# Four products by zero columns in each second block of an attention backward loop

## The chip, the cores and the metric

The kernel runs on one core of one Trainium2 chip. The metric is the device time of one execution, in microseconds. Before the change it is 2607.16 us, the median of 7 runs (2601.39 to 2613.71).

## The reference

The kernel computes a transformer block with adaptive layer norm and all its gradients: attention with 32 heads of 16 over 2048 tokens of width 512, a dense part with a squared ReLU (width 1792), in bfloat16. What matters here is the attention and its gradient:

```
scores = jnp.einsum('bhqd,bhkd->bhqk', q, k) * Dh ** (-0.5)
p = _softmax(scores, axis=-1)
o = jnp.einsum('bhqk,bhkd->bhqd', p, v)
...
_out, _vjp = jax.vjp(_f, A_x, A_wqkv, A_wo, B_w1, B_b1, B_w2, B_b2, c, w_mod)
_grads = _vjp(grad_out)
```

The gradient needs, for each head, dV (the transposed probabilities by dO), dS (the probabilities times dO by V transposed, less a row sum), dK (dS transposed by Q) and dQ (dS by K).

## The kernel before

The program runs three stages: forward (to about 1060 us of the profile), the gradient of the last dense chunk (to about 1180), and from there the backward loop of the attention, to about 2475. A short last stage makes the gradients of the input and of the qkv weights.

The backward loop works in units. A unit is one group of four heads, one stretch of 512 keys and one tile of 128 queries: 8 x 4 x 16 = 512 units. Four units that share their keys and lie in the same stretch of 512 queries are a block; there are 128. In each unit:

- `score` (L1546): for each of four heads a product of 32 rows (a head's 16 values and the row that carries the softmax's correction, padded) by 512 keys, into one of three PSUM banks, A, B or C. Bank C is the tag `px`, which is shared with others.
- `expo` (L1552): ScalarE exponentiates a bank of scores into `E_u`.
- `dp_pair` (L1564, L1566): for two heads TensorE makes dO by V transposed into `psD_u`, and VectorE multiplies that by `E_u` into `dS_u`. There are two such pairs in a unit, so 1024 in the loop.
- `transpose_unit` (L1579): a DMA turns `dS_u` into the tile `dsT`, which dQ needs.
- `k_quad` (L1597) and `v_quad` (L1606): four products each, one for each head, on four column tiles beside each other. They add to dK and dV, which stand in one PSUM bank, `accVK`, in rows 32 x head and on. A bank is summed over the 16 units of a stretch of keys, and then copied out by ScalarE (L1609).
- `dq_quad` (L1624) and `dq_out` (L1637): once for each block, two blocks later, the products for dQ into a bank that again has the tag `px`.

In every second block (`on_pe`) the last unit's `dS_u` is turned by TensorE instead of the DMA: `pe_turn` (L1587) makes eight turns of 128 x 128 into `ptT`, once for each half of the unit. Its bank has the tag `px` too, with one buffer. ScalarE then copies the bank into `dsT` (L1695). The second turn can so begin only when the copy of the first is done, and the next score in bank C only when the copy of the second is done.

The order of the work on TensorE, ScalarE and VectorE in a block is written out by hand as a string of tokens (`order_t` for a block with turns in it, `order_n` for one without): s is a score, e an exponential, D a `dp_pair`, q a `k_quad` or `v_quad` in turn, t a turn, T its copy, d two `dq_quad`, Q a `dq_out`. The loop at L1667 reads the tokens and issues in their order; each engine then works its own queue in order and waits on semaphores. The two strings take turns, so the pattern repeats after two blocks: a pair of blocks, of which there are 64.

The tile `KS_tok` (K by token) is 528 wide; its columns 512 to 527 are set to zero ahead of the loop (L1314), so that the last head's 32-column slice is whole. `dOs_tok` is dO by token.

Of the kernel before, what the change touches and what calls it, by code (L numbers as in the profile page):

```python
# [21 lines left out]
D = 512  # L22
DC = 4
H = 32
DH = 16
# [5 lines left out]
QPAD = 528  # L31
# [3 lines left out]
def kernel(  # L35
# [17 lines left out]
    PE = nc.tensor  # L53
# [91 lines left out]
    with ExitStack() as ph:  # L145
# [1006 lines left out]
        def head_fill(i):  # L1152
            for key in ("k", "v", "q", "do"):
                POOL.memset(hsets[i][key][:], 1.0 if key in ("k", "v") else 0.0)
# [333 lines left out]
    KS_tok, dOs_tok = keep["KS"], keep["dOs"]  # L1488
# [11 lines left out]
    with ExitStack() as ph:  # L1500
# [6 lines left out]
        NU = len(units)  # L1507
        hst, bst, sst, dqt, cur = {}, {}, {}, {}, {}

        def load_head(hg):  # L1510
            st = dict(hsets[hg % 2])
            st["qz"] = qz[hg % 2]
            st["acc"] = stg.tile([P, n], F32, name="dQacc", tag="dQacc", bufs=1)
            st["dq"] = stg.tile([P, n], BF, name="dQst", tag="dQst", bufs=1)
            st["vk"] = stg.tile([P, n], BF, name="vkb", tag="vkb")
            hst[hg] = st
# [22 lines left out]
        def score(u, hq, bank):  # L1539
            hg, kc, qc, qi = units[u]  # L1540
            st = hst[hg]
            qt = qc * 4 + qi
            r = 32 * hq
            psS = psx.tile([P, 512], F32, name=f"psS_{bank}", tag=banks[bank])
            sst[u, hq] = psS
            PE.matmul(psS[:], st["q"][r:r + 32, qt * P:(qt + 1) * P], st["k"][r:r + 32, kc * 512:kc * 512 + 512],  # L1546
                      start=True, stop=True, tile_position=(r, 0))

        def expo(u, hq):
            if hq == 0:  # L1550
                bst[u] = [ework.tile([P, 4, 512], BF, name="E_u", tag="E_u"), None]
            ACT.activation(bst[u][0][:, hq, :], sst.pop((u, hq))[:], AF.Exp, scale=SCALE)  # L1552

        def dp_pair(u, pair):
            hg, kc, qc, qi = units[u]
            st = hst[hg]
            qt = qc * 4 + qi
            if pair == 0:
                bst[u][1] = ework.tile([P, 4, 512], BF, name="dS_u", tag="dS_u", bufs=6)
            E_u, dS_u = bst[u]  # L1560
            psD = psd.tile([P, 2, 512], F32, name="psD_u", tag="pd")
            for hi in range(2):
                r = 32 * (2 * pair + hi)
                PE.matmul(psD[:, hi, :], st["do"][r:r + 32, qt * P:(qt + 1) * P], st["v"][r:r + 32, kc * 512:kc * 512 + 512],  # L1564
                          start=True, stop=True, tile_position=(r, 0))
            DVE.tensor_tensor(dS_u[:, 2 * pair:2 * pair + 2, :], psD[:], E_u[:, 2 * pair:2 * pair + 2, :], ALU.mult)  # L1566
            if qi == 3 and on_pe(u // 4):
                held["dS"] = dS_u

        def on_pe(b):  # L1570
            return b % 2 == 1

        def transpose_unit(u):
            hg, kc, qc, qi = units[u]
            if qi == 0:
                dqt[u // 4] = tpool.tile([P, 4, 16, P], BF, name="dsT", tag="dsT")
            if qi == 3 and on_pe(u // 4):
                return
            SP.dma_start(out=dqt[u // 4][:, qi], in_=bst[u][1].rearrange("p h k -> p (h k)"), transpose=True)  # L1579

        held = {}

        def pe_turn(b, half):
            pt = psx.tile([P, 8, P], BF, name="ptT", tag="px")
            for i in range(8):
                kt = i % 4
                PE.transpose(pt[:, i, :], held["dS"][:, 2 * half + i // 4, kt * P:(kt + 1) * P], identb[:])  # L1587
            dst = dqt[b][:, 3, 8 * half:8 * half + 8, :]
            held[half] = (dst, pt)
# [26 lines left out]
        def dq_quad(b, kt):  # L1616
            hg, kc, qc, _ = units[4 * b]
            if kt == 0:
                cur["dq"] = psx.tile([P, 512], F32, name="dqacc", tag="px")
            acc = cur["dq"]  # L1620
            tT = dqt[b]
            for hq in range(4):
                h = hg * 4 + hq
                PE.matmul(acc[32 * hq:32 * hq + 32, :], KS_tok[:, kc * 4 + kt, h * DH:h * DH + 32], tT[:, :, hq * 4 + kt, :],  # L1624
                          start=(kt == 0), stop=(kt == 3), tile_position=(0, 32 * hq), skip_group_check=True)

        def dq_out(b):
            hg, kc, qc, _ = units[4 * b]
            acc = cur["dq"]
            del dqt[b]  # L1630
            st = hst[hg]
            dst = st["acc"][:, qc * 512:(qc + 1) * 512]
            if kc == 0:
                ACT.activation(dst, acc[:], AF.Identity, scale=SCALE)
            else:
                tmp = wk.tile([P, 512], F32, name="dqtmp", tag="dqtmp")
                ACT.activation(tmp[:], acc[:], AF.Identity, scale=SCALE)  # L1637
                if kc == QC - 1:
                    dst2 = st["dq"][:, qc * 512:(qc + 1) * 512]
                else:  # L1640
                    dst2 = dst
                POOL.tensor_tensor(dst2, dst, tmp[:], ALU.add)  # L1642
            if kc == QC - 1 and qc == QC - 1 and hg < HG - 1:
                for hq in range(4):
                    r = hg % 2 * 64 + hq * DH
                    at(cur["j"] + 6 + hq, load, dQc[hg // 2, r:r + DH, :], st["dq"][32 * hq:32 * hq + DH, :])

        order_t = (
            "s0 s1 q s2 e0 e1 D s3 D e2 s4 e3 t1 e4 q T1 D "
            "s5 s6 e5 t2 e6 s7 T2 e7 D s8 e8 D s9 e9 q q s10 "  # L1650
            "s11 e10 D d1 d2 e11 Q q s12 D e12 s13 e13 q s14 D e14 "
            "s15 q q e15 ").split(), "ABCABBABACABABCA"
        order_n = (
# [9 lines left out]
        with tc.manual_schedule(engines={PE.engine, ACT.engine, DVE.engine, SP.engine, POOL.engine}):  # L1663
            head_fill(1)
            POOL.memset(qz[1][:], 0.0)
            nD, nq = -1, -4
            for b in range(NU // 4 + 3):  # L1667
                toks, bank = order_t if on_pe(b - 1) else order_n
                for tok in toks:
                    c, i = tok[0], int(tok[1:] or 0)  # L1670
                    if c == "s" and b < NU // 4:
                        if i == 0 and units[4 * b][1:] == (0, 2, 0) and units[4 * b][0] + 1 < HG:
                            load_head(units[4 * b][0] + 1)
                        score(4 * b + i // 4, i % 4, bank[i])
                    elif c == "e" and b < NU // 4:
                        expo(4 * b + i // 4, i % 4)
                    elif c == "D":
                        if 0 <= nD < 2 * NU:
                            dp_pair(nD // 2, nD % 2)
                            if nD % 2 == 1:  # L1680
                                transpose_unit(nD // 2)
                        nD += 1
                        cur["j"] = nD
                        for j in sorted(j for j in todo if j <= nD):
                            for f, args in todo.pop(j):
                                f(*args)
                    elif c == "q":
                        if 0 <= nq < 2 * NU:
                            (v_quad if nq % 2 else k_quad)(nq // 2)
                        nq += 1  # L1690
                    elif c == "t" and 0 <= b - 1 < NU // 4:
                        pe_turn(b - 1, i - 1)
                    elif c == "T" and 0 <= b - 1 < NU // 4:
                        dst, pt = held.pop(i - 1)
                        ACT.activation(dst, pt[:], AF.Identity)  # L1695
                    elif c == "d" and 0 <= b - 2 < NU // 4:
                        for kt in (2 * i - 2, 2 * i - 1):
                            dq_quad(b - 2, kt)
                    elif c == "Q" and 0 <= b - 2 < NU // 4:
                        dq_out(b - 2)  # L1700
            assert not todo
# [284 lines left out]
```

## Time and profile before

| what | value |
|---|---|
| median of 7 runs | 2607.16 us |
| the profiled execution | 2607.46 us, of which the profile's span is 2605.7 us |
| TensorE (PE) busy | 2352.8 us, 90% of the span |
| ScalarE (ACT) busy | 2304.6 us, 88% |
| VectorE (DVE) busy | 1809.8 us, 69% |
| the backward loop, first turn's copy to last pair's | 1202.2 to 2473.6 us |
| busy in that stretch of 1271.4 us | PE 1178.1, ACT 1211.5, DVE 1168.3 us |
| TensorE's granted clock in that stretch, mean | 0.93 of full speed |
| the copies of the turns, L1695 | 128 of 1.15 us |
| the turns, L1587 | 1024 products of 128 columns |

A share over the whole span says little here, since the stages have different limits: ahead of the loop VectorE is half idle, and in the loop three engines are each busy for nine tenths or more. In such a loop the order in which they wait for one another sets the time. The profile writes a group of instructions as its line, engine and operation, then output<-inputs; a matmul's form is written rows*columns of the part of the array that it uses, then the moving operand. Durations of matmuls overlap one another: how fast they follow is read from their starts. The clock of TensorE is given as a share of full speed.

### The profile page before, as it was taken

To read this page: it belongs to the slowest core of one execution; us is meant where nothing else is said; L and a number is where in the kernel's file an instruction comes from. 1 tells how busy PE (TensorE), PEld (TensorE's weight loads), DVE (VectorE), ACT (ScalarE), POOL (GpSimd) and SP (SyncE) were. 2 spreads that over 40 slices of the span, in tenths; PEclk is the share of its full clock that TensorE was granted. 3 is DMA by queue.
4 is the path that set the end of the run, shared out by engine and by line. 5 is a ranking of instruction groups with operands and counts; after the bars stand their busy time and mean duration, and the time that the engine had idled before them with its cause. 6 is when DMAs were issued, how large, how long until landed. Compare 5 with 4: busy or idle time off the path is not lost.

```text
span 2605.7 us, 49454 instructions
## 1 busy us (share of the span) xinstructions
PE 2352.8 (90%) x18444; PEld 758.6 (29%) x18444; DVE 1809.8 (69%) x2301; ACT 2304.6 (88%) x3565; POOL 363.6 (14%) x371
## 2 busy tenths in 40 slices
PE   7995989888989889898999999999999999999999
PEld 2231123222322222442222222222222222222243
DVE  5551354445344535579998999899999999999862
ACT  5996999999999999738999999999999999999952
POOL 4000010210242123201111101111011110100100
PEclk8885569997998899999999999899999999999999
DMA  3566565346847674989999999999999999999972
GB/s 130 153 160 172 160 146 134 107 119 130 139 85 150 138 123 93 240 237 198 196 193 193 197 201 200 189 201 195 200 197 197 199 194 197 194 192 209 189 249 73
DMA packets 1227775, 447.49 MB, mean 172 GB/s; under 512 B 1103419, under 2 KB 1198399, under 8 KB 1227278
## 3 DMA queue, kind: packets, MB, share of 16 engines
q1 hardware_dynamic: 1199614, 409.47, 80.1%
q0 software_dynamic: 10944, 16.78, 4.5%
q10 hardware_dynamic: 16976, 18.07, 2.5%
q8 instruction: 145, 2.38, 0.4%
q14 instruction: 96, 0.79, 0.1%
HBM read 96.75 MB, written 73.95 MB: 66 GB/s over the span
## 4 chain that ended last, share of the span: by engine, by line
PE 45%; ACT 36%; issue 6%; DVE 6%; DMA 2%; SPq 2%; POOL 1%; ACTq 0%; DVEq 0%; POOLq 0%
ACT E_u L1552 20%; ACT ET L555 11%; PE dqacc L1624 6%; PE psST L553 4%; PE psS_A L1546 4%; ACT dsT L1695 3%; PE accVK L1597 3%; PE psS_C L1546 3%; PE oacc L569 2%; PE psS_B L1546 2%; PE pm L228 2%; PE accVK L1606 2%; PE pm L393 2%; SPq L173 2%; PE pdh L1810 2%
## 5 line engine op out<-in xcount | busy, mean ns | idle before, releaser
L1566 DVE TENSOR_TENSOR dS_u<-psD_u,E_u 128x1024 bf16<-128x1024 f32 x1024 | 1187.3, 1218 | 105.9 <-PE psS_B L1546 50.7
L555 ACT ACTIVATE ET<-psST 128x1024 bf16<-128x1024 f32 x1024 | 946.4, 1171 | 69.8 <-PE psST L553 69.1
L1552 ACT ACTIVATE E_u<-psS_A 128x512 bf16<-128x512 f32 x768 | 504.4, 657 | 22.2 <-PE psD_u L1564 10.3
L1552 ACT ACTIVATE E_u<-psS_B 128x512 bf16<-128x512 f32 x768 | 500.0, 651 | 6.6 <-PE psS_A L1546 1.7
L1564 PE MATMUL psD_u<-iv,ido 32*128 32x512 bf16 x2048 | 424.1, 399 | 1.7 <-DVE dS_u L1566 1.5
L553 PE MATMUL psST<-qt_sb,kt_sb 32*128 32x512 bf16 x2048 | 353.5, 434 | 70.2 <-ACT ET L555 40.5
L1552 ACT ACTIVATE E_u<-psS_C 128x512 bf16<-128x512 f32 x512 | 333.1, 651 | 0.7 <-PE psS_B L1546 0.5
L1546 PE MATMUL psS_B<-ik,iq 32*128 32x512 bf16 x768 | 306.5, 399 | 10.8 <-ACT E_u L1552 3.4
L1546 PE MATMUL psS_A<-ik,iq 32*128 32x512 bf16 x768 | 304.5, 397 | 11.6 <-ACT E_u L1552 1.3
L569 PE MATMUL oacc<-ET,vaug 128*32 128x512 bf16 x2048 | 232.7, 444 | 5.2 <-DVE ostage L573 5.1
L1597 PE MATMUL accVK<-dS_u,qz 128*32 128x512 bf16 x2048 | 227.8, 414 | 0.3 <-DVE dS_u L1566 0.2
L1546 PE MATMUL psS_C<-ik,iq 32*128 32x512 bf16 x512 | 194.7, 380 | 33.0 <-ACT dsT L1695 29.0
L1546 PEld LDWEIGHTS <-iq 32*128 32x128 bf16 x2048 | 127.5, 92 | 312.1 <-issue 297.6
L1606 PE MATMUL accVK<-E_u,dOs_tok 128*16 128x512 bf16 x2048 | 211.5, 403 | 0.0
L1642 POOL TENSOR_TENSOR dQacc<-dQacc,dqtmp 128x512 f32<-128x512 f32 x64 | 81.2, 1269 | 879.5 <-ACT dqtmp L1637 879.5
L1624 PE MATMUL dqacc<-dsT,KS_tok 128*32 128x512 bf16 x2048 | 183.2, 467 | 12.2 <-DMA dsT<-dS_u 3.0
L553 PEld LDWEIGHTS <-kt_sb 32*128 32x128 bf16 x2048 | 86.7, 93 | 361.1 <-issue 327.2
L246 DVE COPY part<-pm 128x512 f32<-128x512 f32 (+2 forms) x103 | 63.5, 616 | 134.9 <-PE pm L228 131.0
L1695 ACT ACTIVATE dsT<-ptT 128x1024 bf16<-128x1024 bf16 x128 | 147.2, 1150 | 3.6 <-PE ptT L1587 3.6
L1564 PEld LDWEIGHTS <-ido 32*128 32x128 bf16 x2048 | 107.2, 91 | 108.3 <-issue 102.6
L1597 PEld LDWEIGHTS <-qz 128*32 128x32 bf16 x2048 | 61.1, 98 | 242.1 <-issue 229.1
L1587 PE MATMUL ptT<-identb,dS_u 128*128 128x128 bf16 x1024 | 81.3, 224 | 31.7 <-ACT dsT L1695 25.0
(389 smaller groups left out, 2309.9 us busy)
## 6 DMA issues: line engine op xcount, KB each, us to landing
p_st<-part POOLq DMA_DIRECT2D x36, 256.0 KB, 5.3
kt_sb<-qkT_st SPq DMA_DIRECT2D x124, 64.0 KB
wA<-in_B_w_dram SPq DMA_DIRECT2D x28, 256.0 KB
dsT<-dS_u SPq DMA_TRANSPOSE x448
wB<-w1T_st SPq DMA_DIRECT2D x21, 256.0 KB
wA<-w2T_st SPq DMA_DIRECT2D x21, 256.0 KB
wB<-in_B_w_dram SPq DMA_DIRECT2D x21, 256.0 KB
p_st<-part POOLq DMA_DIRECT2D x25, 192.0 KB, 4.1
```

Source lines behind the costliest of these rows:

```text
L553: PE.matmul(ps[:, hi, :], kt_sb[r:r + 32, kt * P:(kt + 1) * P], qt_sb[r:r + 32, :], start=True, stop=True, tile_position=(r, 0))
L555: ACT.activation(ET[:, 2 * pair:2 * pair + 2, :], ps[:], AF.Exp, scale=SCALE)
L569: PE.matmul(oacc[32 * hq:32 * hq + 32, :], lhsT, ET[:, hq, :], start=(kt == 0), stop=(kt == TT - 1), tile_position=(0, 32 * hq), skip_grou ...
L1546: PE.matmul(psS[:], st["q"][r:r + 32, qt * P:(qt + 1) * P], st["k"][r:r + 32, kc * 512:kc * 512 + 512], start=True, stop=True, tile_positi ...
L1552: ACT.activation(bst[u][0][:, hq, :], sst.pop((u, hq))[:], AF.Exp, scale=SCALE)
L1564: PE.matmul(psD[:, hi, :], st["do"][r:r + 32, qt * P:(qt + 1) * P], st["v"][r:r + 32, kc * 512:kc * 512 + 512], start=True, stop=True, til ...
L1566: DVE.tensor_tensor(dS_u[:, 2 * pair:2 * pair + 2, :], psD[:], E_u[:, 2 * pair:2 * pair + 2, :], ALU.mult)
L1587: PE.transpose(pt[:, i, :], held["dS"][:, 2 * half + i // 4, kt * P:(kt + 1) * P], identb[:])
L1597: PE.matmul(cur["vk"][32 * hq:32 * hq + 32, :], hst[hg]["qz"][:, qt, hq, :], bst[u][1][:, hq, :], start=(qt == 0), stop=False, tile_positi ...
L1606: PE.matmul(acc[32 * hq:32 * hq + DH, :], dOs_tok[:, qt, (hg * 4 + hq) * DH:(hg * 4 + hq + 1) * DH], E_u[:, hq, :], start=False, stop=(qt ...
L1624: PE.matmul(acc[32 * hq:32 * hq + 32, :], KS_tok[:, kc * 4 + kt, h * DH:h * DH + 32], tT[:, :, hq * 4 + kt, :], start=(kt == 0), stop=(kt ...
L1695: ACT.activation(dst, pt[:], AF.Identity)
```

## The change

A helper is added, which issues one product: sixteen columns of `KS_tok` that hold zeros as the stationary operand, and a row block of `dOs_tok` (128 rows, 512 columns) as the moving one. It adds to the first sixteen rows of the bank `accVK` that is being summed, with no start and no stop of the sum, so zeros are added to dV of the first head. A new token, f, calls it, and it stands four times in `order_t`: twice ahead of the second turn (t2), and twice ahead of s9, which is the first score in bank C after the copies. The condition leaves it out where no bank is being summed, at either end of the loop, so it is issued 64 x 4 = 256 times.

```diff
+        def keep_warm():
+            PE.matmul(cur["vk"][0:DH, :], KS_tok[:, 0, D:QPAD], dOs_tok[:, 0, :], start=False, stop=False,
+                      tile_position=(0, 0), skip_group_check=True)
+
...
         order_t = (
             "s0 s1 q s2 e0 e1 D s3 D e2 s4 e3 t1 e4 q T1 D "
-            "s5 s6 e5 t2 e6 s7 T2 e7 D s8 e8 D s9 e9 q q s10 "
+            "s5 s6 e5 f f t2 e6 s7 T2 e7 D s8 e8 D f f s9 e9 q q s10 "
             "s11 e10 D d1 d2 e11 Q q s12 D e12 s13 e13 q s14 D e14 "
             "s15 q q e15 ").split(), "ABCABBABACABABCA"
...
+                    elif c == "f" and 0 < nq < 2 * NU:
+                        keep_warm()
```

## The prediction

> **What bounds the kernel now.** I read the page first, then the waits of the backward loop (1200 to 2480 us), its timeline, and tables of busy time by stretch. The loop is half of the span, and the page's costliest group is in it (busy time, mean ns of one | idle time before it, and what ended most of that):
>
> ```profile
> L1566 DVE TENSOR_TENSOR dS_u<-psD_u,E_u 128x1024 bf16<-128x1024 f32 x1024 | 1187.3, 1218 | 105.9 <-PE psS_B L1546 50.7
> ```
>
> VectorE works through 1024 of these, 1187.3/1024 = 1.16 us each, so 16 of them, a pair of blocks, need 18.55 us. That is its floor. TensorE makes it wait. The waits of the loop for TensorE and VectorE (us in total, times, longest):
>
> ```profile
> PE psS_C L1546 <- ACT dsT L1695: 29.0, 62, 0.5
> PE ptT L1587 <- ACT dsT L1695: 25.0, 58, 0.4
> ...
> DVE dS_u L1566 <- PE psS_B L1546: 50.5, 44, 1.6
> DVE dS_u L1566 <- PE psD_u L1564: 17.4, 35, 1.6
> ```
>
> The first two are the places where the products are added: TensorE waits for ScalarE to copy a turned tile out of the shared bank px. They are short, yet VectorE's waits are up to 1.6 us. The timeline of TensorE in one pair (start, duration in us) shows what lies between:
>
> ```profile
> 1806.05 0.39 PE L1564 MATMUL psD_u<-iv,ido 32*128 32x512 bf16 x2
> 1806.17 0.37 PE L1546 MATMUL psS_B<-ik,iq 32*128 32x512 bf16 x1
> 1806.28 0.37 PE L1546 MATMUL psS_A<-ik,iq 32*128 32x512 bf16 x1
> 1807.08 0.61 PE L1587 MATMUL ptT<-identb,dS_u 128*128 128x128 bf16 x8 [0.43 <-ACT dsT L1695]
> ...
> 1808.11 0.39 PE L1564 MATMUL psD_u<-iv,ido 32*128 32x512 bf16 x2
> 1808.98 0.37 PE L1546 MATMUL psS_C<-ik,iq 32*128 32x512 bf16 x1 [0.48 <-ACT dsT L1695]
> 1809.28 0.62 PE L1597 MATMUL accVK<-dS_u,qz 128*32 128x512 bf16 x4
> 1809.68 0.64 PE L1606 MATMUL accVK<-E_u,dOs_tok 128*16 128x512 bf16 x4
> ```
>
> After the second wait the same products take 0.62 us instead of 0.40. Stretches of 3.41 us, in which the granted clock changes (busy us of PE, PEld, DVE, ACT, POOL with counts, then the granted clock), from this pair and, in the second fence, from a pair that kept its clock:
>
> ```profile
> 1805.86:1809.27 3.41, 2.45 (x23) 0.97 (x19) 3.33 (x3) 3.41 (x7) 0.00 (x0) 0.99 1.14 124
> 1809.27:1812.68 3.41, 3.41 (x33) 0.84 (x32) 2.55 (x3) 2.22 (x5) 0.00 (x0) 0.51 1.17 243
> 1812.68:1816.10 3.42, 3.33 (x44) 0.92 (x37) 2.68 (x3) 3.29 (x7) 1.27 (x1) 1.00 0.84 162
> ```
>
> ```profile
> 1464.48:1467.89 3.41, 2.45 (x27) 0.90 (x23) 3.25 (x4) 3.41 (x7) 0.00 (x0) 1.00 1.16 210
> 1467.89:1471.31 3.42, 3.26 (x40) 1.05 (x36) 3.05 (x3) 3.42 (x9) 0.74 (x1) 1.00 1.09 208
> ```
>
> The window that holds both waits is followed by one at half clock. VectorE loses 0.86 us in it (2.55 of 3.41). Such windows begin at 47 places of the loop, mostly 20.48 us, six windows, apart. The same columns for two pairs of blocks without (nearly) and two with:
>
> ```profile
> 1464.00:1483.30 19.30, 17.70 (x180) 5.63 (x176) 18.49 (x17) 19.23 (x38) 2.53 (x2) 1.00 1.15 197
> 1483.30:1502.80 19.50, 17.85 (x180) 5.84 (x176) 18.79 (x17) 19.28 (x38) 2.55 (x2) 0.98 1.12 182
> 1805.90:1826.30 20.40, 18.94 (x180) 5.66 (x176) 18.58 (x17) 19.00 (x38) 2.54 (x2) 0.92 1.14 183
> 1826.30:1846.70 20.40, 18.94 (x180) 5.67 (x176) 18.54 (x17) 19.50 (x39) 2.54 (x2) 0.92 1.05 187
> ```
>
> From first turn copy to first turn copy, pairs at full clock take 19.1 to 19.5 us (1464.0 to 1502.8: 19.37 each), pairs with a slow window 20.4.
>
> **What makes the clock fall.** Plain busy time doesn't separate the windows: 2.45 us stands in one that is followed by half clock and in one that isn't. I counted each product by the array rows that its tile uses: a 128-row product or a turn as 1, a 32-row one as a quarter, over the time that it streams (0.213 us for 512 columns: full-row groups start 0.22 to 0.23 us apart). For 1805.86 to 1809.27: the second turn 0.43 us and a remnant of a quad 0.07 count in full, eleven 32-row products give 11 x 0.053 = 0.59; 1.09/3.41 = 0.32. Over all 319 full-clock windows of the loop, those below about 0.377 are followed by a slow one and those above are not, with one exception. This is an estimate from the trace's rows; it says that the waits matter because they leave out full-row work, not by their length.
>
> A rule that speaks against the change is in the Trainium skill, TensorE: Matmul & The Clock Gate, "Why this matters for your kernels": gaps must stay under some 3 us between bursts for the clock to hold (one idle window lowers it). The longest gap here is 0.48 us. By that rule no window of this loop should be slow and filling gaps buys nothing: 2607 plus what the products cost. The row decides: half clock follows gaps of 0.43 and 0.48 us. The same page, "A second HAM failure mode: psum-queue depth-cycling", allows for it. I go by the row.
>
> **The change part by part.** Nothing is removed or moved. 256 products (128 rows x 16 zero columns, moving 512) with 256 weight loads are added to TensorE's queue alone, four in each of 64 pairs: two ahead of the second turn, two ahead of psS_C, which are the two waits above. The order of the other queues and their DMAs is the same, and none of the new products has a wait of its own.
>
> *Their price.* The form 128*16 stands in L1606, but there four run beside each other on four column tiles; the new ones share one tile, so they stream one after the other, 0.22 us each. Going from 32-row to 128-row work takes about 0.31 us start to start, and back 0.32 (1814.93 to 1815.25, 1815.48 to 1815.80). First pair: 1806.28 + 0.31 + 0.22 + 0.22 = 1807.03, and the turn started at 1807.08. Second: 1808.11 + 0.31 + 0.22 + 0.32 = 1808.96, against 1808.98. Both fit, by 0.05 and 0.02 us; ScalarE's copies hide them. This is what they cost if the cover is gone: all four at full clock 0.88 us, at half clock 1.7 us. If the weight load of each second product isn't hidden (PEld of L1606: 87 ns), 0.1 us per pair of products shows, on the path, since everything behind psS_C is queued on TensorE and VectorE already waits 0.37 us there in a pair at full clock (1470.32). Ends: 0 (a product can't hasten a copy) and 2 x 0.18 x 63 = 23 us; I take 0.05 us a pair of blocks, 3 us, near the lower end, for the two sums above fit.
>
> *What they bring.* By the count above each adds 0.213 us in full. Window 1805.86 to 1809.27 rises from 0.32 to (1.09 + 0.85)/3.41 = 0.57; one that holds only one pair of products gains 0.12. Moving the window over a full-clock pair with the products put in, one position stays under 0.377: a window that ends 0.8 to 0.5 us ahead of the first turn copy, where mostly 32-row scores run. The windows from 1498.61 and 1983.31 behave so now, without any such wait in them. That band is 0.26 us of 3.41, so 7% of pairs by chance: 63 x 0.07 = 4 to 5 slow windows left instead of 47, at about 0.5 us (19.87 for the pair at 1502.8, against 19.37) to 1 us: 4 us.
>
> *The sum.* From 1202.2 to 2473.6 us there are 63 pairs, 1271.4 us, 20.18 on average. At full clock 63 x 19.37 = 1220.3, a gain of 51. Less 4 for slow windows left and 3 for friction: 44. What is late next: VectorE at 18.55 us, ScalarE busy 19.2 of 19.3; so no more than a few us beyond 51. Ahead of the loop and behind it nothing changes. The profiled execution took 2607.46 us (span 2605.7 and 1.8 around it), 0.3 above the median of 2607.16, so both give **2563 us**, -1.7%.
>
> **Rivals.** (a) *The clock holds, as above*: 2552 to 2575. For it: the count fits 318 of 319 windows. Chance 0.73.
> (b) *A new lock.* The slow windows had fixed themselves to the loop: a pair at 20.4 is nearly six windows. Three pairs at 19.35 are 58.05 us, nearly 17 windows (58.03), so a phase can stick. If the pair becomes 19.4 to 19.45 and a slow window costs 1 us, stepping the pairs against the windows gives about 23 slow ones and a loop of 1246: 2607 - 25 = 2582, between 2575 and 2602. Against: those seen cost 0.5. Chance 0.14.
> (c) *The clock ignores the products, and TensorE pays* (slower). If zero weights, or 16 columns, don't count, the 20.4 us pairs stay. Then the fill-ins delay the second turn and psS_C by 0.1 us each where the weight load shows, 2 x 0.1 x 64 = 13: 2620; up to 2640 if 0.2 each and in the slow windows more. It decides from where the delay exceeds the gain: with the gain gone, from any delay over 0.08 us a pair (5 us); with it, only from 0.8 us a pair. For: the trace has no product with zero weights. Chance 0.10.
> (d) *Nothing*: (c) with full cover, within 5 us. Chance 0.03.
>
> **Numbers.** 0.2% is 5 us, about what a measurement can tell here. (a) and (b) are faster, 0.87; same 0.03; slower 0.10. The range 2552 to 2601 leaves out (c) and the ends of the others, some 0.18.
>
> **What would show it.** In the profile after: granted clock of the loop 0.98 or more instead of 0.93; pairs of blocks at 19.3 to 19.45 us; VectorE's waits for psS_B and psD_u from 68 us to under 30; the waits of ptT and psS_C for the copy nearly gone, with psS_C not later than 3.15 us behind the first copy (now 3.1). Wrong if half-clock windows stay 20.48 us apart, if they move to the end of the block's scores in every third pair (b), or if VectorE's gap ahead of the dq products grows past 0.37 us (friction).

## The result and the profile after

The changed kernel takes 2593.87 us (median of 13 runs, 2587.24 to 2601.58); the kernel before, run beside it, 2607.08 (34 runs). The ratio is 0.9949, 95% interval 0.9936 to 0.9961: faster by 13 us, where 44 were forecast. The profiled execution took 2588.75 us (span 2587.0). The backward loop, first turn's copy to last pair's, went from 1271.4 to 1251.4 us (1201.0 to 2452.4).

The added products do where they stand what was said of them. TensorE's timeline of one pair after the change (start, duration, as before; the helper has moved the lines behind it: L1584 is the added product, L1591 the turn, L1601 and L1610 the two quads, L1628 the products for dQ, L1701 the copy of a turn):

```profile
1297.57 0.37 PE L1546 MATMUL psS_B<-ik,iq 32*128 32x512 bf16 x1
1297.68 0.37 PE L1546 MATMUL psS_A<-ik,iq 32*128 32x512 bf16 x1
1297.98 0.60 PE L1584 MATMUL accVK<-dOs_tok,KS_tok 128*16 128x512 bf16 x2
1298.51 0.62 PE L1591 MATMUL ptT<-identb,dS_u 128*128 128x128 bf16 x8
...
1299.52 0.39 PE L1564 MATMUL psD_u<-iv,ido 32*128 32x512 bf16 x2
1299.84 0.60 PE L1584 MATMUL accVK<-dOs_tok,KS_tok 128*16 128x512 bf16 x2
1300.38 0.37 PE L1546 MATMUL psS_C<-ik,iq 32*128 32x512 bf16 x1
1300.69 0.40 PE L1601 MATMUL accVK<-dS_u,qz 128*32 128x512 bf16 x4
```

No wait is written at the second turn or at psS_C, and psS_C starts 3.10 us behind the first copy of the turns (1297.28), as before. The quad behind it takes 0.40 us, not 0.62. The windows of the kernel after (length, then busy us of PE, PEld, DVE, ACT, POOL with counts, then granted clock, DMA share, GB/s) are the loop, two ordinary pairs and one at a change of head group:

```profile
1202.20:2460.00 1257.80, 1197.49 (x11383) 371.61 (x11382) 1167.07 (x1007) 1209.34 (x2297) 140.01 (x102) 0.97 1.17 200
1297.30:1316.60 19.30, 18.66 (x184) 5.84 (x180) 18.49 (x17) 19.23 (x38) 2.54 (x2) 1.00 1.19 206
1316.60:1336.00 19.40, 18.70 (x186) 5.91 (x183) 18.70 (x17) 19.18 (x38) 2.54 (x2) 1.00 1.17 190
1355.10:1380.40 25.30, 22.17 (x184) 5.77 (x180) 19.14 (x17) 19.60 (x37) 0.00 (x0) 0.80 1.16 194
```

The clock holds: 0.97 in the loop against 0.93, and 12 stretches of half clock (65 us in all) where there were 47 (177 us). The median pair went from 20.39 to 19.33 us. But six of the 63 pairs take 23.1 to 25.3 us, together 144.5, and 6 x 19.33 = 116.0 would do: 28.5 us. They begin at 1355.1, 1515.3, 1836.1, 1994.5, 2153.1 and 2352.5, five of them at a change of the group of heads and the last two pairs behind one. The loop of this execution won 20 us where 44 were forecast, so these six pairs hold the gain that is missing. The timeline in the first of them:

```profile
1355.10 0.33 ACTq L1528 DMA_DIRECT2D iqs<-q_st  x1
...
1363.78 0.35 ACTq L1528 DMA_DIRECT2D iqs<-q_st  x1
1364.23 0.60 ACT L1552 ACTIVATE E_u<-psS_A 128x512 bf16<-128x512 f32 x1 [2.44 <-DMA dsT<-dS_u]
1364.73 0.59 ACT L1552 ACTIVATE E_u<-psS_B 128x512 bf16<-128x512 f32 x1
1364.88 0.58 PE L1546 MATMUL psS_A<-ik,iq 32*128 32x512 bf16 x1 [2.54 <-ACT E_u L1552]
1365.20 0.60 ACT L1552 ACTIVATE E_u<-psS_C 128x512 bf16<-128x512 f32 x1
1365.35 1.23 DVE L1566 TENSOR_TENSOR dS_u<-psD_u,E_u 128x1024 bf16<-128x1024 f32 x1 [2.29 <-ACT E_u L1552]
```

ScalarE has to issue a load (iqs, at 1363.78), and the exponential behind it starts 2.44 us late. What released it is a turning DMA (dsT<-dS_u). TensorE and VectorE then stand still for want of ScalarE, and the psS_A at 1364.88 already runs at half clock (0.58 us). So a long pair pays twice, for the stall and for the clock that falls behind it: by the clock's records half clock lasts 10.2 us from 1364.4 on, and 44 of the loop's 65 us of half clock lie in the six long pairs, each time within the stall or right behind it. Outside them 6 stretches (21 us) are left. The waits of the loop after the change (us in total, times, longest) have this in them:

```profile
DVE dS_u L1566 <- PE psD_u L1564: 22.7, 46, 1.2
DVE dS_u L1566 <- ACT E_u L1552: 16.5, 13, 3.0
DVE dS_u L1566 <- PE psS_B L1546: 14.6, 29, 1.8
...
ACT E_u L1552 <- DMA dsT<-dS_u: 11.2, 4, 3.3
...
PE dqacc L1628 <- ACT E_u L1552: 9.4, 3, 3.5
```

VectorE's waits for psS_B and psD_u fell from 68 to 37 us, and the two waits for the copies are gone from the list. The three waits shown whose longest is 3 us or more, at L1566, L1552 and L1628, were not among those that carried the argument. ScalarE's (L1552) ends with a turning DMA in four of the six long pairs, and the other two wait for ScalarE; in a fifth long pair, from 1836.1, the records show ScalarE's load held back until 1843.28 by a turn in the same way.

That leads to one queue: SyncE's, which issues the turning DMAs (L1579) one after the other. Its row gives the time of an issue, which is called a turn's time here; the data land 5.3 us (median) after the issue began. Worked out from the starts and ends of its 440 issues in the loop: before, the queue had 59 us of gaps, so seven turns, a pair's, took 7 x (1271.4 - 59)/440 = 19.3 us of a pair of 20.2. After, the gaps are 17 us, and seven turns take 7 x (1251.4 - 17)/440 = 19.6 us, more than the 19.33 that a pair now wants. The turns fall behind VectorE: half of them start 1.3 us or more after their dS_u is ready in the kernel before, and 3.0 us or more in the kernel after. In the pair from 2296 us it is 0 to 1.3 us, two pairs later, ahead of the last long pair, 3.8 to 8.2 us. A long pair doesn't need such a lag, though: in the first one it is 0 to 3.5 us, and the turn that holds the load up (issued at 1355.94 beside stores of dQ) takes 7.8 us to land.

### The profile page after: what moved, and what is told of

The parts are those of the page before. It is cut to its first block, busy times and chain, and to the rows that moved or that the text cites. A ratio compares the mean times of both kernels' runs of the same rounds, so it can differ in the third digit from the quotient of the medians.

```text
span 2587.0 us, 49966 instructions
## 1 busy us (share of the span) xinstructions
PE 2371.2 (92%) x18700; PEld 772.4 (30%) x18700; DVE 1809.4 (70%) x2301; ACT 2299.6 (89%) x3565; POOL 364.3 (14%) x371
## 4 chain that ended last, share of the span: by engine, by line
PE 41%; ACT 37%; issue 7%; DVE 7%; DMA 5%; SPq 2%; POOL 1%; ACTq 0%; DVEq 0%; POOLq 0%
ACT E_u L1552 22%; ACT ET L555 12%; PE dqacc L1628 4%; PE psST L553 4%; PE psS_A L1546 3%; PE oacc L569 2%; DMA dsT<-dS_u 2%; PE accVK L1601 2%; PE psS_B L1546 2%; PE pm L228 2%; ACT dsT L1701 2%; PE pm L393 2%; PE psS_C L1546 2%; PE pdh L1816 2%; PE accVK L1610 2%
## 5 line engine op out<-in xcount | busy, mean ns | idle before, releaser
L1566 DVE TENSOR_TENSOR dS_u<-psD_u,E_u 128x1024 bf16<-128x1024 f32 x1024 | 1186.8, 1218 | 86.4 <-PE psD_u L1564 23.5
L1552 ACT ACTIVATE E_u<-psS_A 128x512 bf16<-128x512 f32 x768 | 509.2, 663 | 16.0 <-DMA d_st<-dltT 7.2
L1552 ACT ACTIVATE E_u<-psS_B 128x512 bf16<-128x512 f32 x768 | 502.6, 654 | 8.7 <-PE psD_u L1564 4.3
L1564 PE MATMUL psD_u<-iv,ido 32*128 32x512 bf16 x2048 | 412.7, 390 | 2.4 <-DVE dS_u L1566 2.0
L1552 ACT ACTIVATE E_u<-psS_C 128x512 bf16<-128x512 f32 x512 | 333.3, 651 | 13.0 <-DMA dsT<-dS_u 8.8
L1546 PE MATMUL psS_A<-ik,iq 32*128 32x512 bf16 x768 | 295.9, 385 | 16.0 <-ACT E_u L1552 6.0
L1546 PE MATMUL psS_B<-ik,iq 32*128 32x512 bf16 x768 | 296.9, 387 | 10.6 <-ACT E_u L1552 3.4
L1601 PE MATMUL accVK<-dS_u,qz 128*32 128x512 bf16 x2048 | 215.6, 394 | 0.7 <-DVE dS_u L1566 0.4
L1610 PE MATMUL accVK<-E_u,dOs_tok 128*16 128x512 bf16 x2048 | 205.6, 391 | 0.0
L1628 PE MATMUL dqacc<-dsT,KS_tok 128*32 128x512 bf16 x2048 | 150.9, 394 | 25.8 <-ACT E_u L1552 9.4
L1701 ACT ACTIVATE dsT<-ptT 128x1024 bf16<-128x1024 bf16 x128 | 145.4, 1136 | 7.7 <-PE ptT L1591 7.4
L1601 PEld LDWEIGHTS <-qz 128*32 128x32 bf16 x2048 | 58.4, 94 | 183.8 <-issue 169.6
L569 PEld LDWEIGHTS <-vaug 128*32 128x32 bf16 x2048 | 54.5, 95 | 150.6 <-issue 150.6
```

The lines of the kernel that those rows point to most:

```text
L569: PE.matmul(oacc[32 * hq:32 * hq + 32, :], lhsT, ET[:, hq, :], start=(kt == 0), stop=(kt == TT - 1), tile_position=(0, 32 * hq), skip_grou ...
L1601: PE.matmul(cur["vk"][32 * hq:32 * hq + 32, :], hst[hg]["qz"][:, qt, hq, :], bst[u][1][:, hq, :], start=(qt == 0), stop=False, tile_positi ...
L1610: PE.matmul(acc[32 * hq:32 * hq + DH, :], dOs_tok[:, qt, (hg * 4 + hq) * DH:(hg * 4 + hq + 1) * DH], E_u[:, hq, :], start=False, stop=(qt ...
```

## The experiments

Theory T: the pairs are now faster than SyncE's queue of turns; it falls behind through a group of heads, and whatever first waits for an old turn pays. Its rivals are named in the expectations; H puts the loss on the issue of loads and stores from ScalarE's queue. Where an expectation takes 2.83 us for a turn (19.8 for seven), that is the mean issue of 2.71 and 0.12 between two; the sum above, without an assumed distance, gives 19.6.

**One turn of seven less.** The third unit of each odd block isn't turned; GpSimd sets its part of dsT to zero, so that dQ lacks it. Once in the changed kernel (a_six), once in the one before (b_six):

```diff
         def transpose_unit(u):
...
+            if qi == 2 and on_pe(u // 4):
+                POOL.memset(dqt[u // 4][:, qi], 0.0)
+                return
```

> The changed kernel with six turning DMAs for a pair of blocks instead of seven: the third unit of each odd block isn't turned, GpSimd sets its part of dsT to zero, so dQ lacks that unit. Theory T: SyncE needs 6 x 2.83 = 17 us for a pair, the lag stays under 3 us, no stall at head changes, 2560 to 2568. Theory H: ScalarE's DMA issues wait for late turns, which aren't late now, so also about 2566. Theory F (the products themselves or the slow windows left are the loss): no gain, 2588 to 2594.

> The kernel before with six turning DMAs for a pair instead of seven (the third unit of each odd block is left out of dQ as in a_six). Theories T and H: the queue has slack in the kernel before and the clock sets its pair at 20.4 us, so within 6 us of 2607. Half-clock windows stay, 40 to 50.

Measured: a_six 2557.44 us, ratio to before 0.9815 (0.979 to 0.9839); b_six 2599.86, 0.9974 (0.9957 to 0.9992). The loop of a_six, in the columns of the windows above:

```profile
1200.00:2426.50 1226.50, 1184.73 (x11337) 364.22 (x11335) 1164.92 (x1009) 1206.27 (x2296) 249.53 (x164) 0.98 1.03 177
```

With six turns the same four products bring 42 us, and no pair takes over 21 us (51 of 63 are under 19.6). In the kernel before, the same relief brings 7. Both times lie just under what was expected: a_six 2.6 us below T's range (H expects nearly the same here), b_six 7 us below 2607 instead of at most 6. F falls. So the products bring nearly what was forecast once a turn is out of the way, and the rest was lost in the turns. The new memsets are work on an engine that is mostly idle; they would make a_six slower, if anything.

**Less beside the turns.** The per-head loads of q, k, v and dO are left out for the groups 3 to 7 of the eight, counted from 0, which compute on the data of the groups 1 and 2 (a_noload, and b_noload on the kernel before):

```diff
             for i, (to, fro) in enumerate(loads):
-                at(j0 + 4 * i, load, to, fro)
+                if hg < 3:
+                    at(j0 + 4 * i, load, to, fro)
```

> The changed kernel with the per-head loads of q, k, v and dO for the heads 3 to 7 of 8 left out (those groups compute on the data of the groups 1 and 2). Theory T with the other transfers as what lengthens a turn: the mean issue of a turning DMA in the groups 2 to 6 falls from 2.71 to 2.6 us or less, the queue's demand to 19.0 us or less for a pair, and of the pairs above 21 us those that pay the debt of these groups go: at most three left, 2568 to 2582 us. Theory T with the turn's own length alone: mean 2.68 to 2.75 us, the stalls only move, 2586 to 2598 us. Rival C (clash of stores and loads): at most two stalls left, 2565 to 2575 us, with the mean issue unchanged.

> The kernel before the change with the same per-head loads left out (heads 3 to 7 of 8; those groups compute on the data of groups 1 and 2). Theory T: in the kernel before SyncE's queue has 59 us to spare in the loop and its turns are not what a pair waits for, so leaving the loads out brings little: 2600 to 2610 us, slow clock stretches 45 to 48, although the mean issue of a turn falls from 2.65 to 2.6 us or less. Rival E (the loads hold up ScalarE or the other engines wherever they stand, queue or not): it gains about what it gained in the changed kernel, 2578 to 2590 us.

Measured: a_noload 2569.97 us, 0.9853 (0.982 to 0.9886); b_noload 2603.51, 0.9977 (0.9964 to 0.999). The turning issues of the loop's middle, 1520 to 2160 us (count, then shortest, median and longest in ns, then first and last start), for the kernel after and then for a_noload, where one added line makes L1579 L1580:

```profile
L1579 SPq DMA_TRANSPOSE dsT<-dS_u x225: 1622/2663/4399, 1519.7 to 2157.7; - x113
```

```profile
L1580 SPq DMA_TRANSPOSE dsT<-dS_u x230: 1684/2484/4166, 1517.4 to 2158.5; - x115
```

The median turn is 0.18 us shorter, and five more fit into the same 640 us. The mean by group of heads is 2.53 to 2.59 us in the groups 3 to 6, during which no load runs, against 2.71 to 2.73 in the kernel after; in the first two groups, in which loads still run, it is 2.64 and 2.74, against 2.62 and 2.69. (Group 2, in which the loads for group 3 would run, has 2.67 against 2.75.) One pair above 21 us is left. So T holds in its first form: other transfers lengthen a turn. Rival C's time (2565 to 2575) fits too, but not its unchanged turns. In the kernel before, where the queue had room, the same cut brought 7 us, as T expected, so rival E falls.

**Where the debt is paid.** a_late begins the loads later in the group and spreads the stores of dQ; a_buf has two more buffers of dS_u.

```diff
-            j0 = (hg - 1) * 128 + 14
+            j0 = (hg - 1) * 128 + 34
...
-                    at(cur["j"] + 6 + hq, load, dQc[hg // 2, r:r + DH, :], st["dq"][32 * hq:32 * hq + DH, :])
+                    at(cur["j"] + 6 + 6 * hq, load, dQc[hg // 2, r:r + DH, :], st["dq"][32 * hq:32 * hq + DH, :])
```

```diff
-                bst[u][1] = ework.tile([P, 4, 512], BF, name="dS_u", tag="dS_u", bufs=6)
+                bst[u][1] = ework.tile([P, 4, 512], BF, name="dS_u", tag="dS_u", bufs=8)
```

> The changed kernel with the per-head loads begun 20 pairs of products later in the head (34 instead of 14 after its start) and the four stores of dQ six pairs apart instead of one. Theory T (SyncE's queue of turning DMAs, 7 x 2.83 = 19.8 us for a pair of blocks of 19.3 us, falls behind all through a head, and the debt is paid wherever something first waits for an old turn): the place of the payment moves, its sum stays, 2588 to 2600 us with four to seven pairs above 21 us. Rival C (the loss comes of the clash of stores and loads with each other at the head change, not of the queue's rate): the stalls go, 2563 to 2573 us with at most one pair above 21 us.

> The changed kernel with eight buffers of dS_u instead of six. Theory T: a buffer more only lets the queue fall further behind before VectorE waits; the debt is still collected by the wait of ScalarE's DMA issues and of the dQ products, 2588 to 2600 us. Rival D (the number of buffers of dS_u is what limits, and the queue's mean rate suffices): VectorE's waits for turning DMAs and the long pairs go, 2563 to 2575 us.

Measured: a_late 2593.86 us, 0.9942 (0.9923 to 0.9962), five pairs above 21 us; a_buf 2591.7, 0.9934 (0.9912 to 0.9956), six. The time stays and the place moves. A wait of the loop of a_late (columns as before) that the kernel after hardly has:

```profile
DVE dS_u L1566 <- DMA dsT<-dS_u: 17.9, 20, 2.0
```

VectorE now waits for a buffer of dS_u that a late turn still reads. In a_buf ScalarE's wait behind its DMA issues is 16.1 us instead of 11.2. Rivals C and D fall.

**Another queue for loads and stores.** All of L1528's transfers go to GpSimd's queue (a_pool; b_pool on the kernel before), or to SyncE's, among the turns (a_sp, on the changed kernel).

```diff
         def load(to, fro):
-            ACT.dma_start(out=to, in_=fro)
+            POOL.dma_start(out=to, in_=fro)
```

> The changed kernel with the loop's loads and stores (L1528) issued by GpSimd in place of ScalarE; nothing is left out. Theory H (ScalarE stands at its own DMA issues where a head changes, and that alone is the loss): the six stalls of 4 to 6 us go, the pairs stay at 19.3 us, some 28 us are won: about 2566. Theory T (SyncE's queue of turning DMAs is full, 7 x 2.83 = 19.8 us for a pair of 19.3; the head change is only the place where the debt is paid): ScalarE's waits for a DMA go, the lag of the turns behind VectorE grows past 8 us instead, the dQ products wait for their DMA, and the time stays at 2583 to 2594.

> The kernel before with the loop's loads and stores issued by GpSimd in place of ScalarE; nothing is left out. Both theories: in the kernel before the turns keep up and the head changes cost little, so within 5 us of 2607.

> The changed kernel with the loop's loads and stores issued by SyncE, in the queue of the turning DMAs; nothing is left out. Theory H: ScalarE's stalls go, about 2566. Theory T with the issue on SyncE as the limit: 28 issues of 0.34 us more for a head, 10 us, so 2620 to 2660. Theory T with the transfers themselves as the limit: 2585 to 2605.

Measured: a_pool 2613.28 us, 1.0029 (1.001 to 1.0048); b_pool 2617.62, 1.0035 (1.0017 to 1.0053); a_sp 2645.61, 1.015 (1.0105 to 1.0194). In a_pool ScalarE's wait for a turning DMA is gone from the waits of the loop, but these two are there:

```profile
PE psD_u L1564 <- DVE dS_u L1566: 26.7, 27, 3.8
DVE dS_u L1566 <- DMA dsT<-dS_u: 25.4, 18, 4.4
```

Theory H, for which the stall goes with the issue and 28 us are won, falls. Both kernels are slower than expected, a_pool by 19 us, and b_pool 10 us above before instead of at most 5: with the loads and stores on this queue turns have a mean of 2.77 us in both, and in a_pool the queue has 6 us of gaps left. Why they are longer is not shown. a_sp shows that SyncE's queue has no room: putting the loads into it costs 52 us against the changed kernel's 2593.87, as T with the issue on SyncE as the limit expected.

**Which of the four products.** a_first keeps only the two ahead of the second turn, a_second only the two ahead of psS_C, and a_second32 only these, with 32 rows instead of 128.

```diff
-            "s5 s6 e5 f f t2 e6 s7 T2 e7 D s8 e8 D f f s9 e9 q q s10 "
+            "s5 s6 e5 f f t2 e6 s7 T2 e7 D s8 e8 D s9 e9 q q s10 "
```

```diff
-            "s5 s6 e5 f f t2 e6 s7 T2 e7 D s8 e8 D f f s9 e9 q q s10 "
+            "s5 s6 e5 t2 e6 s7 T2 e7 D s8 e8 D f f s9 e9 q q s10 "
```

```diff
-            PE.matmul(cur["vk"][0:DH, :], KS_tok[:, 0, D:QPAD], dOs_tok[:, 0, :], start=False, stop=False,
+            PE.matmul(cur["vk"][0:DH, :], KS_tok[0:32, 0, D:QPAD], dOs_tok[0:32, 0, :], start=False, stop=False,
```

> Only the two products ahead of the second turn. Row theory: 0.44 as well, the clock holds nearly as in the changed kernel, 10 to 20 slow windows, 2588 to 2600. If only the last wait ahead of the slow window counts: over 35 slow windows, 2600 to 2610.

> Only the two products ahead of psS_C (the first pair of them is left out, no result is changed). Row theory (a window under 0.377 of full-row work is followed by half clock): the window with both waits stands at 0.32 + 0.125 = 0.44, so the clock holds nearly as in the changed kernel, 10 to 20 slow windows in the loop, time 2588 to 2600. If both places are needed: over 35 slow windows and 2600 to 2610.

> The two products ahead of psS_C use 32 rows instead of 128, for the same time. Row theory: they add a quarter, 0.32 + 0.03 = 0.35, still under 0.377: 35 to 50 slow windows, 2602 to 2612. Theory that busy time alone counts: the same as with 128 rows ahead of psS_C, 10 to 20 slow windows.

Measured: a_first 2597.06 us, 0.9957 (0.9938 to 0.9976), 11 stretches of half clock; a_second 2592.35, 0.9942 (0.9922 to 0.9962), 8, even fewer than expected; a_second32 2591.59, 0.9941 (0.9921 to 0.9961), 19. Two products do what four do. What was expected of a_second32 (35 to 50 stretches, 2602 to 2612 us) was missed, and its 19 stretches are what the rival theory of busy time alone had named: even 32-row products move most windows over the mark. The rule itself held there: with a 32-row product as a quarter and the mark at 0.377, it names 18 of the 19 windows that are followed by half clock, and hardly another; counting such a product in full names fewer than half of them. The times of these three can't rank the versions, since the turns limit all of them.

## Why the prediction was wrong

The step that failed is "What is late next: VectorE at 18.55 us, ScalarE busy 19.2 of 19.3; so no more than a few us beyond 51". It lists the engines and no queue: the DMA queue was put at nothing, and all that is said of it is that its order stays the same. SyncE's turns needed 19.3 us for a pair already before, by the gaps of that trace, and the forecast pair was 19.37: the next limit was less than 0.1 us away, and a turn only had to become less than 1% longer to pass it. It became 2% longer (a mean of 2.65, then 2.71 us). What that costs stands in four pairs of kernels:

| in a pair of blocks | without the products | with them | gain |
|---|---|---|---|
| seven turns, all loads and stores on GpSimd's queue | 2617.62 | 2613.28 | 4 |
| seven turns, all loads | 2607.08 | 2593.87 | 13 |
| seven turns, loads of five groups left out | 2603.51 | 2569.97 | 34 |
| six turns | 2599.86 | 2557.44 | 42 |

The rows were run at different times; by the ratios to before the gains are 2 (within the noise), 13, 32 and 41. The more the turns are relieved, the more the same products bring.

A second look at before could have warned. The transfers of the loop stretch (packets, MB, rate) of before, after, a_noload and a_six, in this order:

```profile
DMA packets 929902, 250.03 MB, mean 197 GB/s; under 512 B 920299, under 2 KB 926827, under 8 KB 929763
```

```profile
DMA packets 928015, 249.59 MB, mean 199 GB/s; under 512 B 918410, under 2 KB 924938, under 8 KB 927874
```

```profile
DMA packets 921661, 242.65 MB, mean 197 GB/s; under 512 B 915936, under 2 KB 919904, under 8 KB 921520
```

```profile
DMA packets 798560, 216.95 MB, mean 177 GB/s; under 512 B 788954, under 2 KB 795482, under 8 KB 798418
```

The same bytes in the forecast loop of 1220.3 + 7 = 1227.3 us would be 249.6 MB / 1227.3 us = 203 GB/s. No kernel here moved more than 200 over its loop; at 199 or 200, 249.6 MB take 1248 to 1254 us, which is what the loop took. That is a warning and no hard ceiling: of 40 equal slices of the loop of the kernel after, one reaches 214. a_six, with 177, isn't held by its transfers. A page of the Trainium skill, DMA: Bandwidth & Descriptors (Latency and other measured facts), gives a transposing DMA 261 GB/s or more. A turn here is 128 x 2048 values of two bytes, 0.524 MB: at that rate an estimated 2.0 us, and a queue with room to spare. The row has a median of 2.66 us, so 197 GB/s; only 86 of the 448 turns of the kernel after were as short as that. The measurement decides.

Point by point:

- *The clock falls by the rows in a window*: right. 47 slow windows became 12, and the mark of 0.377 held in kernels that it wasn't drawn from. The rule of long gaps, which the prediction set against its count, would have left 2607. The count's 0.213 us for 512 columns is 0.215 to 0.227 in the trace of before (start to start of the products for dQ), which changes nothing here.
- *The price of the products, 0.05 us a pair*: none is seen. The median pair is 19.33 us, and those at full clock took 19.37 before.
- *Slow windows left, 4 to 5*: 6 outside the long pairs, and 11 in a_six, where no stall adds any. The cost was close nevertheless: the loop of a_six is 1226.5 us, 63 x 19.33 = 1217.8 and 9 on top, where 4 and 3 were taken for windows and friction.
- *The sum, 44*: 42 with six turns. With seven, 28.5 of it went into six pairs.
- *The signs*: pairs at 19.3 to 19.45 us and psS_C at 3.10 came; clock 0.98 became 0.97 and the waits 37 instead of under 30. None of them looked at the queue.
- *Rivals*: (c) and (d) fall, and so does (b), a new lock: its loss would be spread over every third pair, while 47 of 63 are under 19.6 us. The loss had a cause that no rival named.

What stays open is how much of the limit is the rate of the 16 DMA engines and how much the one queue that issues turn after turn: fewer turns and fewer other bytes both relieve it. Where the queue had more to issue, in a_sp, it was the queue: over the loop, at 192 GB/s, 440 turns (2.47 us on average) and 206 loads and stores (0.75) filled 1243 of 1304.5 us. None of the versions that compute everything beats the changed kernel by more than their intervals: the best, a_second32 and a_buf, are 2 us below it.

## What to carry to other kernels

When a stall goes, compare the new rhythm with every queue's own need, not only with the engines': sum the issues of the DMA queue over one turn of the loop, and divide the loop's bytes by its forecast time. A queue that is 95% full in a loop with stalls is the limit of the loop without them. To test a gain that didn't come, take load off the suspected resource in both kernels, with and without the change: if the changed one gains far more (here 24 to 36 us against 4 to 7), the resource was holding it.

## What the runs showed of the hardware

- An issue on ScalarE can stop its arithmetic: the load at 1363.78 made the exponential 2.44 us late, released by a turning DMA of another queue. In the records of this program, loads and turns take their semaphores from one set in turn, so a load may wait for a turn that it has nothing to do with.
- One stall can cost the clock as well: with stalls of 1.3 to 3.3 us, or right behind them, TensorE ran at half clock for 3.4 to 10.2 us in all six long pairs.
- A turn's time depends on what moves beside it: in the groups 3 to 6 of the changed kernel 2.53 to 2.59 us without loads and 2.71 to 2.73 with them, over the loop 2.77 with them on GpSimd's queue. It depends on the pace too: 2.60 to 2.62 with the loads in the same groups of the slower kernel before.
- Sixteen columns of zeros hold the clock like other work: two such products of 128 rows in a pair of blocks took the slow stretches from 47 to 8 or 11, by their place, two of 32 rows to 19.
